# RWKV-7 recurrence feeding a GELU MLP on one core: r's load and transpose are moved, and one chunk's first MLP product changes its tile shape

## The chip, the cores and the metric

The kernel runs on one core of a Trainium2 chip. The metric is the device time of one execution in microseconds; the time of a kernel is the median of several runs. The engines are named as in the profile: PE is TensorE's matmuls and PEld its weight loads, DVE is VectorE, ACT ScalarE, POOL GpSimd, SP SyncE, which here issues nearly all DMAs.

## The reference

For each of 4 batches and 8 heads, a 40x40 state runs through 768 time steps:

```
y[t]  = r[t] @ state
Sa    = state @ a[t]
state = state * w[t] - outer(Sa, b[t]) + outer(v[t], k[t])
```

The 8 heads' y (8 x 40 = 320 columns) become the rows of x, 3072 tokens by 320. Then `h = x @ w_in` (320 to 2048), `g = gelu(h)` with erf, and `out = g @ w_out` (2048 to 320). Everything is float32.

## The kernel before

The 768 steps are cut into 12 chunks, c = 0 to 11, of C = 64 steps. Inside a chunk the recurrence is turned into small matrix products: N and A (a against b and k), M and RV (r against sa and v), an inverse of a unit triangular 64x64 block (a 32x32 part of it on POOL, column by column, L682 and L684; the rest as the products J on PE), X (state against a), saT, and QY (outputs and new state together). All 32 batch and head pairs of a chunk are done at once: 64 products of 40 or 64 rows each, four at a time in 64x64 tiles of the array, or 16 in 32x32 tiles for J.

The order of work is written out by hand. The instructions of each engine run in the order in which the Python code emits them. The loop `for c in range(2, NCH)` at the end of the function is one turn per chunk. In turn c the code finishes chunk c (corner, make_X, joined, make_saT, sa_blocks, make_y2, make_M, make_QY, outputs), prepares chunk n = c + 1 (make_A, make_av, make_RV) and loads and prepares chunk n2 = c + 2 (logs, sums, scale_a, turn_b, turn_r, make_N, the start of its inverse). Turns 3 to 9 have a chunk n2 and take the `else` branches that the diff edits.

Between these steps stand calls of `fill()`. Each runs the next piece of the MLP of the chunk before: mlp(c) is put into the list `pieces` in turn c, so that the first product of mlp(2) is done in turn 3. A chunk's MLP covers 256 tokens (4 batches of 64). The first product, L1043, comes in four pieces, each of 40 matmuls and one GELU over 128x1024 (L1045, ACT):

```
for s in range(2):
    for kt in range(NK):
        for to, end in ((0, HP), (HP, P)):
            for x in range(2):
                matmul(ph[to:end, x, s], w_in_sb[half(x), kt, p*P+to : p*P+end], xt[half(x), kt], ...)
```

NK = 5, HP = 64, P = 128. `half(x)` are the array's upper or lower 64 rows (partitions 0 to 63, 64 to 127), `to` the left or right 64 columns: four 64x64 tiles. Each matmul streams 256 columns. A float32 matmul and its weight load stand in the profile as two records each, so one piece is 80 records and a chunk 320. The second product is L1059 for chunks 0 to 2 and L995 (`seven`, a scheme with seven products of 128x128 tiles) from chunk 3 on; the sums that `seven` needs are DVE work (L1009, L1015, L1016, L999).

What is loaded for chunk n2 in a turn, by SP in this order: w (load_w, 4 DMAs into w_tile, L197), b a second time in the paired form (fetch_pairs "b_turned", 4 DMAs into the a_pairs buffer, L181), r (load_r, 8 DMAs into r_pairs, L178), v (8 DMAs into v_pairs, L178). Then follow the chunk's xt copies (L924, L927), b and k in rows (L163), the inverse's parts (L709, L712), N's store (L620) and its reload for POOL (L674), a and the paired k for the next turn, another copy of v (L217) and the output's stores. b_turned may only start when turn_a has read a_pairs, r when turn_k has read r_pairs, v when turn_v has read v_pairs; these are DVE transposes of 128x1024 (L186). w is read first by logs (ACT's Ln, L425). Within SP a DMA that has to wait holds up all behind it.

turn_r is the DVE transpose r_pairs to rT (L186), from where chunk n2's RV, M and y2 products read it one and two turns later; rT has two buffers. On DVE the turn goes: X's sum (L831), turn_a, turn_k, sa's transpose and 8 copies (L866, L872), the mask of M (L580), turn_v, scale_kT (L547), then the MLP's input xt and the new state (L916, L938, L939), which need QY from PE, then the mask of A, scale_a (L513), turn_b (L186, L522), turn_r, the MLP's sums, the mask of N (L580), L's transpose (L783) and the state's (L952).

Of the kernel before, what the change touches and what calls it, by code (L numbers as in the profile page):

```python
# [19 lines left out]
def kernel(  # L20
# [46 lines left out]
    nc = tc.nc  # L67
    B, H, S, D = r.shape
    DM, DF = moe_w_in.shape
    P = 128  # L70
    C = 64
    HP = 64
# [93 lines left out]
    def fetch_pairs(c, n, src, eng, placed, t=None):  # L166


        if t is None:
            t = paired[n]  # L170
        rows = slice(c * C // 2, (c + 1) * C // 2)
        for x in range(2):
            for z, cols in enumerate((slice(0, D + BL), slice(BL, BW))):
                to = t[x * HP + z * BL:x * HP + (z + 1) * BL, :, :cols.stop - cols.start]
                if placed:
                    for e in range(2):
                        pairs = src[G * e + x].rearrange("h (s y) d -> s h (y d)", y=2)
                        eng.dma_start(out=to[:, e::2], in_=pairs[rows, :, cols])  # L178
                else:
                    pairs = src.rearrange("b (i x) (s y) d -> x s (b i) (y d)", x=2, y=2)[x]  # L180
                    eng.dma_start(out=to, in_=pairs[rows, :, cols])  # L181
        raws[c, n] = t
# [6 lines left out]
    def load_w(c, t=None, eng=nc.sync):  # L189
        t = w_tile if t is None else t  # L190
        to = t[:, :G * DM].rearrange("p (g h d) -> p g h d", g=G, h=H)
        if c < NB:
            fetch(c, "w", w, eng, to)
        else:
            for e in range(2):
                for g in range(G):
                    eng.dma_start(out=to[half(e ^ g), g],  # L197
                                  in_=w[G * e + g, :, c * C:(c + 1) * C].rearrange("h t d -> t h d"))
        raws[c, "w"] = t
# [23 lines left out]
    def load_r(c, eng=nc.sync):  # L223
        if c >= NT:
            fetch_pairs(c, "r", r, eng, True)
            return
        t = by_64(paired["v" if c == 1 else "r"]).rearrange("p (h g) d -> p h g d", g=G)
        for e in range(2):
            for g in range(G):
                eng.dma_start(out=t[half(e), :, g, :D],  # L230
                              in_=r[G * e + g, :, c * C:(c + 1) * C].rearrange("h t d -> t h d"))
        raws[c, "r"] = t
# [311 lines left out]
    def scale_kT(c):  # L544
        t = turned_in[c]
        kT, en = t.pop("k_turned"), t.pop("en")
        nc.vector.tensor_tensor(en, kT, en, ALU.mult)  # L547
        t["kT"] = parts_by_batch(en)
# [485 lines left out]
    def mlp(c):  # L1034
        xt = xts.pop(c)
        for q in range(NF // 4):
            ph = duo("ph").rearrange("p x (s t) -> p x s t", s=2)
            for s in range(2):
                p = 2 * q + s
                for kt in range(NK):  # L1040
                    for to, end in ((0, HP), (HP, P)):
                        for x in range(2):
                            nc.tensor.matmul(ph[to:end, x, s], w_in_sb[half(x), kt, p * P + to:p * P + end],  # L1043
                                             xt[half(x), kt], start=kt == 0, stop=kt == NK - 1)
            nc.scalar.activation(gt[:, 4 * q:4 * q + 4].rearrange("p (x s) t -> p x s t", x=2), ph, ACT.Gelu)  # L1045
            yield
        if c >= NS:
            s1, s2 = half_tile("conv", 2), None
            nc.vector.tensor_tensor(s1, block(1, 0), block(1, 1), ALU.add)  # L1049
            if c >= NCH - 2:  # L1050
                s2 = half_tile("conv", 2)
                nc.vector.tensor_tensor(s2, s1, block(0, 0), ALU.subtract)
            yield from seven(c, s1, s2)
            return
        po = duo("po")[:, :, :DM]
        for part in range(2):
            for g in range(G):
                for f in range(NF // 2 * part, NF // 2 * (part + 1)):
                    nc.tensor.matmul(po[:, g], gt[:, f, g * P:(g + 1) * P], w_out_sb[:, f],  # L1059
                                     start=f == 0, stop=f == NF - 1)  # L1060
                for last in range(G if part and g else 0):
                    os = work.tile([P, DM], FP32, tag="os", name="os", bufs=2)
                    nc.vector.tensor_copy(os, po[:, last])
                    for e in range(2):
                        row = (G * e + last) * S + c * C
                        nc.sync.dma_start(out=out[row:row + C], in_=os[half(e)])
                yield
# [225 lines left out]
    for c in range(2, NCH):  # L1293
        n, n2, n3 = c + 1, c + 2, c + 3
        more, more2, more3 = n < NCH, n2 < NCH, n3 < NCH
        corner(c)
        make_X(c)
        if c > 2:
            turn_blocks(range(4, 16))
        if c == NS + 1:  # L1300
            weight_sums(3)
        if c == 2:

            seconds(1, (14, 14), last=True)
            fill()
            turn_b(n)
            make_N(n)
            run(start_inverse(n, nc.gpsimd))
            store_inverse(n, (nc.gpsimd,))
            load_r(n)  # L1310
            load_v(n)
            load_next(n2)
        else:
            fill()
            if more2:
                load_w(n2)
        joined(c)
        if c == 2:
            pieces.reverse()
            seconds(2, last=True)  # L1320
            fill()
            make_sa(c)
            make_saT(c)
            turn_r(n)
            scale_k(n, nc.vector)
            fill()
            pieces.reverse()
            fill(2)
            turn_k(n)
            load_r(n2)  # L1330
            turn_a(n2)
            fetch_pairs(n2, "b_turned", b, nc.sync, False, paired["a"])
        else:
            if more2:
                turn_a(n2)
                fetch_pairs(n2, "b_turned", b, nc.sync, False, paired["a"])
            if more:
                turn_k(n)
            if more2:
                load_r(n2)  # L1340
            if c == 3:
                scale_b(n)
                scale_k(n, nc.vector)
            fill()
            make_saT(c)
            sa_blocks(c, range(12))
        fill()
        if c > 2:
            sa_blocks(c, range(12, 16))
        make_y2(c)  # L1350
        make_M(c)
        if more:
            turn_v(n)
            if more2:
                load_v(n2)
        if more and c > 2:
            scale_kT(n)
        fill()
        if more2:
            logs(n2)  # L1360
        make_QY(c)
        outputs(c)
        if more2 and c == 2:
            turn_r(n2)
            fetch_pairs(n2, "k_turned", k, nc.sync, False, paired["r"])
        elif more2:
            load_kb(n2)
        pieces.append(mlp(c))
        fill()
        if c == NS:  # L1370
            weight_sums(0)
            weight_sums(1)
        if more:
            make_A(n)
        if more2:
            sums(n2)
        if c > NS:
            fill()
        if more:
            fetch_inverse(n, (0,))  # L1380
            make_av(n)
        if more2:
            scale_a(n2)
            turn_b(n2)
            if c > 2:
                turn_r(n2)
        fill()
        if c == NS:
            weight_sums(2)
        if more2:  # L1390
            make_N(n2)
        if more:
            fetch_inverse(n, (1, 2))
            make_RV(n)
        if more2:
            if c > 2:
                scale_b(n2, nc.gpsimd)
                scale_k(n2, nc.gpsimd)
            steps = start_inverse(n2, nc.gpsimd)
            if more3:  # L1400
                load_a(n3)
            if c == 2:
                load_kb(n2)
            else:
                fetch_pairs(n2, "k_turned", k, nc.sync, False, paired["r"])
            load_VR(n2)
            run(steps)
            store_inverse(n2, (nc.gpsimd,))
        if more:
            if 'early' in ['sm', 'tn']:  # L1410
                turn_within()
                turn_corner(n)
            else:
                turn_corner(n)
                turn_within()
            turn_blocks(range(4))
        fill()
        fill()
# [31 lines left out]
```

## Time and profile before

| | us |
|---|---|
| median of 3 runs (695.57 to 702.57) | 696.25 |
| the profiled execution | 692.65 |
| its span | 690.9 |
| PE busy | 644.9 |
| PEld busy | 557.4 |
| DVE busy | 394.6 |
| POOL busy | 381.9 |
| ACT busy | 286.0 |

The profiled execution's 692.65 us is 1.75 us over its span. The turns of the loop begin with the products X, at 220.2 us for turn 3, 271.1 for turn 4, then 320.5, 370.0, 419.0, 467.3, 516.3 (turn 9), 566.1 and 612.7 (turn 11); they are read from the timeline. The granted clock of TensorE is 1.00 from 200 us to the end. Busy matmul time includes matmuls that overlap each other. "Issue" as a releaser is time in which an engine waited for nothing that the profile shows.

### The profile page before, as it was taken

What the parts mean: (1) busy time and instruction counts of PE and PEld (TensorE: products, weight loads), DVE (VectorE), ACT (ScalarE), POOL (GpSimd) and SP (SyncE); (2) the same over time, 40 slices, a digit from 0 to 9 for tenths busy, and PEclk for the clock granted to TensorE, in tenths of its full rate; (3) what the DMA queues carried; (4) which work ended last, traced back from release to release, by engine and by line L of the source; (5) the groups of instructions that cost most, each with busy time, mean ns of one, the idle gap of its engine ahead of it and who ended that gap; (6) DMA issues with size and microseconds to landing.
All of it is one profiled execution on the core that took longest, in us unless ns stands there. A gap on an engine that the chain in (4) does not pass through costs nothing.

```text
span 690.9 us, 35541 instructions
## 1 busy us (share of the span) xinstructions
PE 644.9 (93%) x16050; PEld 557.4 (81%) x16050; DVE 394.6 (57%) x548; ACT 286.0 (41%) x523; POOL 381.9 (55%) x812
## 2 busy tenths in 40 slices
PE   7578898889999999999999999999999999999997
PEld 4467787657777876898997998997998889979977
DVE  2325779994253774675674684774775765623403
ACT  5223675444143443444445435426526425143020
POOL 5375458820861865855845866875866847820000
PEclk9885899889999999999999999999999999999999
DMA  9698648664658759639649657557657564030100
GB/s 129 109 175 147 128 91 208 139 132 93 124 99 142 130 95 145 116 74 154 123 80 154 127 93 151 112 98 142 116 102 147 104 112 84 23 56 4 39 2 20
DMA packets 287935, 74.64 MB, mean 108 GB/s; under 512 B 265736, under 2 KB 284456, under 8 KB 287784
## 3 DMA queue, kind: packets, MB, share of 16 engines
q1 hardware_dynamic: 283360, 68.20, 54.2%
q0 software_dynamic: 864, 2.36, 2.3%
q8 instruction: 126, 2.06, 1.3%
q10 hardware_dynamic: 3560, 1.80, 1.0%
q14 instruction: 25, 0.20, 0.1%
HBM read 58.69 MB, written 9.70 MB: 99 GB/s over the span
## 4 chain that ended last, share of the span: by engine, by line
PE 73%; POOL 10%; issue 4%; SPq 4%; DVE 3%; DMA 3%; ACT 1%; ACTq 0%; POOLq 0%; DVEq 0%
PE ph L1043 26%; PE po L995 17%; PE po L1059 7%; PE QY L110 6%; POOL W L684 4%; POOL tmp L682 4%; PE J L110 2%; SPq L163 2%; PE sq L110 2%; PE N_ps L110 2%; PE M_ps L110 2%; PE av L110 2%; PE A_ps L110 2%; PE saT_ps L110 2%; PE RV_ps L110 1%
## 5 line engine op out<-in xcount | busy, mean ns | idle before, releaser
L1043 PE MATMUL ph<-xt,w_in_sb 64*64 64x256 f32 x3840 | 222.5, 378 | 5.5 <-issue 5.0
L1043 PEld LDWEIGHTS ph<-xt,w_in_sb 64*64 64x64 f32 x3840 | 169.1, 133 | 41.0 <-issue 9.8
L682 POOL TENSOR_TENSOR tmp<-W,Nb 128x126 f32<-128x126 f32 (+22 forms) x310 | 126.1, 407 | 96.9 <-DMA Nb<-N 73.3
L684 POOL TENSOR_TENSOR W<-W,tmp 128x126 f32<-128x126 f32 (+22 forms) x310 | 133.8, 432 | 24.3
L1045 ACT ACTIVATE gt<-ph 128x1024 f32<-128x1024 f32 x48 | 49.2, 1024 | 108.4 <-PE ph L1043 108.3
L995 PE MATMUL po<-w_out_sb,gt 128*128 128x160 f32 x576 | 84.7, 303 | 0.0
L995 PEld LDWEIGHTS po<-w_out_sb,gt 128*128 128x128 f32 x576 | 78.9, 190 | 4.9 <-issue 3.3
L963 ACT COPY turned<-within 32x256 f32<-32x256 f32 (+3 forms) x144 | 46.3, 322 | 56.0 <-DVE within L952 54.3
L1059 PE MATMUL po<-w_out_sb,gt 128*128 128x320 f32 x192 | 55.7, 447 | 0.0
L1059 PEld LDWEIGHTS po<-w_out_sb,gt 128*128 128x128 f32 x192 | 36.7, 195 | 15.6 <-issue 1.6
L637 POOL TENSOR_TENSOR VR<-VR,upper 128x1024 f32<-128x1024 f32 x8 | 18.9, 2366 | 43.1 <-ACT VR L636 38.4
L916 DVE TENSOR_TENSOR xt<-QY,wpT 128x512 f32<-128x512 f32 x24 | 15.5, 687 | 40.4 <-PE QY L110 40.0
L872 DVE COPY SM<-sa 32x256 f32<-32x256 f32 x72 | 33.5, 465 | 1.2
L814 DVE COPY Tt<-J 32x512 f32<-32x512 f32 x9 | 6.2, 689 | 41.6 <-PE J L110 41.6
L320 ACT ACTIVATE conv<-conv,rebias 128x320 uint32<-128x320 uint32 (+1 forms) x26 | 16.1, 624 | 29.0 <-DVE conv L319 25.9
L995 PE MATMUL po<-extra,half 128*128 128x160 f32 x176 | 26.1, 303 | 0.0
L783 DVE STREAM_TRANSPOSE L<-Tt 128x512 f32<-128x512 f32 x11 | 7.8, 710 | 30.3 <-DMA Tt<-inv 30.3
L866 DVE STREAM_TRANSPOSE sa<-saT 128x1024 f32<-128x1024 f32 x9 | 11.2, 1245 | 23.5 <-ACT saT L856 23.5
L995 PEld LDWEIGHTS po<-extra,half 128*128 128x128 f32 x176 | 24.2, 190 | 0.3
L872 ACT COPY SM<-sa 32x64 f32<-32x64 f32 x72 | 17.4, 242 | 12.8 <-DVE sa L866 11.8
L1049 DVE TENSOR_TENSOR half<-gt 128x1024 f32<-128x1024 f32 x9 | 11.8, 1313 | 18.3 <-ACT gt L1045 18.3
L995 PE MATMUL po<-extra,gt 128*128 128x160 f32 x144 | 21.0, 299 | 0.0
(233 smaller groups left out, 1151.7 us busy)
## 6 DMA issues: line engine op xcount, KB each, us to landing
Nb<-N SPq DMA_DIRECT2D x20, 256.0 KB
VR<-in_v_dram SPq DMA_DIRECT2D x24, 160.0 KB
out_dram<-os SPq DMA_DIRECT2D x48, 80.0 KB
b_rows<-in_b_dram SPq DMA_DIRECT2D x22, 160.0 KB
k_rows<-in_k_dram SPq DMA_DIRECT2D x22, 160.0 KB
N<-N SPq DMA_DIRECT2D x44, 64.0 KB
Tt<-inv SPq DMA_DIRECT2D x44, 64.0 KB
a_pairs<-in_a_dram SPq DMA_DIRECT2D x18, 144.0 KB
```

The source lines that it names most:

```text
L110: nc.tensor.matmul(o, lhsT, rhs, start=first, stop=True, skip_group_check=True)
L320: nc.scalar.activation(power, power, ACT.Relu, bias=rebias, scale=8.0)
L637: nc.gpsimd.tensor_tensor(to, to, upper.unsqueeze(1).to_broadcast([P, 2 * G * NP, C]), ALU.mult)
L682: eng.tensor_tensor(t, W[:, :rows, j:j + 1].to_broadcast([P, rows, rest]), Nb[:, j:j + 1, j + 1:].to_broadcast([P, rows, rest]), ALU.mult)
L684: eng.tensor_tensor(W[:, :rows, j + 1:], W[:, :rows, j + 1:], t, ALU.add)
L872: copy(t["SM"][to:to + BL, g].rearrange("p q m c -> p (q m) c")[:, :, d * BL:end], t["sa"][at:at + BL, :, to:to + end - d * BL])
L916: nc.vector.tensor_tensor(xt[:, :NP, g * P:(g + 1) * P].rearrange("p i (e t) -> p i e t", e=2), Y, wp[:, g, :, :, :C], ALU.mult)
L963: nc.scalar.copy(tn[to:to + deep, :, at:at + wide], within[0][at:at + deep, :, to:to + wide])
L995: nc.tensor.matmul(po[:, n, :DM // 2], l_[:, f], r_[:, f], start=f == 0, stop=f == NF // 2 - 1)
L1043: nc.tensor.matmul(ph[to:end, x, s], w_in_sb[half(x), kt, p * P + to:p * P + end], xt[half(x), kt], start=kt == 0, stop=kt == NK - 1)
L1045: nc.scalar.activation(gt[:, 4 * q:4 * q + 4].rearrange("p (x s) t -> p x s t", x=2), ph, ACT.Gelu)
L1059: nc.tensor.matmul(po[:, g], gt[:, f, g * P:(g + 1) * P], w_out_sb[:, f], start=f == 0, stop=f == NF - 1)
```

## The change

Three edits, and one that only removes a branch never taken (`'early' in ['sm', 'tn']` is false):

1. In mlp, for c == 2 alone, the two 64-column halves of the weights are one matmul of 128 columns: tiles of 64 rows by 128 columns, two of them (x = 0, 1), in place of four of 64x64. The chunk's first product has 160 records in place of 320, and as many fewer weight loads.
2. In turns 3 to 9, the loads are issued in the order r, w, b_turned in place of w, b_turned, r. load_w no longer stands before joined(c).
3. In turns 3 to 9, turn_r(n2) stands behind scale_kT(n), ahead of the MLP's input in DVE's order, in place of behind turn_b(n2).

```diff
@@ mlp
-                    for to, end in ((0, HP), (HP, P)):
+                    for to, end in ((0, P),) if c == 2 else ((0, HP), (HP, P)):
@@ turn c, after make_X
         else:
             fill()
-            if more2:
-                load_w(n2)
         joined(c)
@@
         else:
             if more2:
                 turn_a(n2)
-                fetch_pairs(n2, "b_turned", b, nc.sync, False, paired["a"])
             if more:
                 turn_k(n)
             if more2:
                 load_r(n2)
+                load_w(n2)
+                fetch_pairs(n2, "b_turned", b, nc.sync, False, paired["a"])
@@
         if more and c > 2:
             scale_kT(n)
+            if more2:
+                turn_r(n2)
         fill()
         if more2:
             logs(n2)
@@
         if more2:
             scale_a(n2)
             turn_b(n2)
-            if c > 2:
-                turn_r(n2)
         fill()
@@
         if more:
-            if 'early' in ['sm', 'tn']:
-                turn_within()
-                turn_corner(n)
-            else:
-                turn_corner(n)
-                turn_within()
+            turn_corner(n)
+            turn_within()
             turn_blocks(range(4))
```

In the order of instructions of each engine nothing else moves: POOL and ACT keep theirs, DVE has the one transpose moved in each of the seven turns, SP the eight loads of r put ahead of the eight of w and b. r's first load then waits for turn_k; the waits of the others keep their sources.

## The prediction

> **What bounds the kernel now.** I read the page's engine lines first, then the chain that ended last, then busy time by turn, then the waits of PE, and last the timelines of one turn for PE, DVE and SP.
>
> ```profile
> span 690.9 us, 35541 instructions
> PE 644.9 (93%) x16050; PEld 557.4 (81%) x16050; DVE 394.6 (57%) x548; ACT 286.0 (41%) x523; POOL 381.9 (55%) x812
> ...
> PE 73%; POOL 10%; issue 4%; SPq 4%; DVE 3%; DMA 3%; ACT 1%; ACTq 0%; POOLq 0%; DVEq 0%
> ```
>
> PE is busy for 93% of the span and makes 73% of the chain. The table by turn (columns: length, then busy time per engine, clock, DMA share, GB/s) shows that this holds in every turn that the change touches.
>
> ```profile
> 220.20:271.10 50.90, 49.89 (x1229) 39.79 (x1228) 31.56 (x38) 22.06 (x43) 34.74 (x70) 1.00 0.72 123
> ...
> 370.00:419.00 49.00, 48.29 (x1278) 43.07 (x1276) 31.49 (x43) 23.07 (x47) 34.19 (x70) 1.00 0.70 122
> ...
> 516.30:565.00 48.70, 47.99 (x1209) 42.69 (x1208) 30.11 (x41) 22.79 (x46) 32.77 (x68) 1.00 0.65 120
> ```
>
> PE is idle for 1.0 us of turn 3, 0.7 of turn 6 and 0.7 of turn 9; over turns 3 to 10 (220.2 to 614.0) the same table sums to 384.9 busy of 393.8, so 8.9 us. What can be won by better waits is bounded by that. The waits of PE, first from 220 to 560 us, then to the end:
>
> ```profile
> PE ph L1043 <- issue: 5.0, 6, 1.6
> ...
> PE J L110 <- DVE L L783: 1.7, 2, 1.2
> ```
>
> In the first stretch PE never waits there for DVE, ACT or a load: its largest entry is "issue", in ph. Only at the end, at 566 and 612 us, does it wait for L, which closes POOL's inverse for the last chunks.
>
> The timelines of turn 6 show where the moved transpose lies (DVE) and where the moved loads lie (SP):
>
> ```profile
> 391.45 1.19 DVE L547 TENSOR_TENSOR en<-k_turned,en 128x1024 f32<-128x1024 f32 x1
> 396.44 1.29 DVE L916 TENSOR_TENSOR xt<-QY,wpT 128x512 f32<-128x512 f32 x2 [3.80 <-PE QY L110]
> ...
> 408.40 1.24 DVE L186 STREAM_TRANSPOSE rT<-r_pairs 128x1024 f32<-128x1024 f32 x1
> ...
> 412.03 1.22 DVE L580 TENSOR_TENSOR N<-N_ps,upper 128x1024 f32<-128x1024 f32 x1
> ```
>
> ```profile
> 382.75 3.16 SPq L197 DMA_DIRECT2D w_tile<-in_w_dram  x4
> 386.00 2.17 SPq L181 DMA_DIRECT2D a_pairs<-in_b_dram  x4
> 388.27 4.66 SPq L178 DMA_DIRECT2D r_pairs<-in_r_dram  x8
> 393.02 4.52 SPq L178 DMA_DIRECT2D v_pairs<-in_v_dram  x8
> ```
>
> DVE stands idle for 3.80 us ahead of xt, waiting for QY; SP issues without a gap.
>
> **The change, part by part.** The sum is made against the profiled execution, 692.65 us (span 690.9 and 1.75 around it). The median of the runs shown is 696.25, 3.6 above it; I carry the difference over.
>
> *The 64x128 tiles (turn 3, on the path).* The same product, undisturbed, is seen in the tail, and the dense 128x128 product beside it:
>
> ```profile
> 653.75 17.43 PE ph L1043 x320
> 671.18 15.43 PE po L995 x112
> ```
>
> 320 records in 17.43 us are 54.5 ns each, so four tiles beside one another stream 256 columns in 218 ns, and a chunk has 80 such slots. In the new shape two tiles have to stream the same 256 columns per slot, and there are again 80 slots: half the records, each covering twice the columns of weights. A dense stream of 128x128 tiles takes 15.43/112 = 138 ns for 160 columns, and the po of turn 3 takes 4.50/16 = 281 ns for 320: 0.86 and 0.88 ns per column, 220 and 225 ns for 256. So a slot is 218 to 225 ns if the two row halves run together, 17.4 to 18.0 us for the chunk, +0 to +0.6; I take +0.1, since the 64x64 row is the nearest (same operands, same row halves). A gain below 218 isn't shown by any row; as a lower end I take -0.2.
>
> The neighbours of these four pieces (X, saT, y2 with M, QY) stay in 64x64 tiles, so the array's shape now changes six more times: after X, before and after saT, before y2, after M, before QY (the J after the first piece changes it anyway). What a change costs is read from equal groups of 64 records in the chain:
>
> ```profile
> 300.48 1.09 PE A_ps L110 x64
> 301.57 0.95 PE wT_ps L110 x64
> ...
> 320.47 1.08 PE X L110 x64
> ```
>
> A_ps follows a 128x128 product, X follows 32x32 tiles, wT_ps follows 64x64 tiles: 0.13 to 0.14 us per change. Six are +0.8. Bounds: 0, if matmul ends hide it, and 1.9, by the gap that J2 makes in turn 3 (the first piece ends at 225.61, the next begins at 226.98, less 0.75 for 64 records of J: 0.31 per change).
>
> *turn_r ahead of xt.* Seven transposes of 1.24 us move into the idle time between en's end and xt's start: 3.47, 3.33, 3.54, 3.80, 3.27, 3.72 and 4.04 us in turns 3 to 9, all over 1.24. That costs nothing while r has landed. In the trace r's eight loads land 7.2 us after the first is issued in turn 6 (388.27 to 395.45). Issued at w's old time, 382.75, they land at 390.0; en ends at 392.64. In turn 9 it is 529.91 + 6.3 = 536.2 against 539.09, in turn 8 487.5 against 490.11. The old reader of that rT buffer, M, is masked on DVE before. Without that cover, xt, the state and X would be late by what r is late beyond about 2.1 us, the room that is left. At its old place the transpose frees 1.2 us ahead of the MLP's sums and N's mask. PE waits for neither: m3 starts right behind RV. The mask comes earlier by up to 1.2 us where DVE was late with it (turn 4: N_ps is done at 312.1, the mask starts at 313.41), but N's store on SP then waits for the fetch of Tt ahead of it: it gains 1.1 us in turn 4, 0.3 in turn 6, nothing in turns 7 to 9, where the store comes 1.7 to 2.5 us behind the mask. What of that reaches the wait for L at the end I put at -0.2 (bounds -1.7, the whole wait, and 0).
>
> *r ahead of w and b on SP.* The same 16 issues; w and b each go out 4.7 to 5.9 us later, the length of r's issues. w landed at 388.05 in turn 6, now at about 392.7; Ln starts at 395.86. In turn 9 it is 537.94 + 4.7 = 542.6 against 542.28, so Ln is 0.3 us late, and behind it on ACT stand the table load and the exponentials, which wait for wT on PE; wT (546.7) has 3.7 us of room behind Ln's end. b lands at 544 instead of 539.5 there, and turn_b starts at 552.6. r's first load now waits for turn_k with w, b, v, xt and N's store queued behind it: SP gets to it after turn_k's end in all turns but turn 4 (280.52 against 282.43, 1.9 us), where SP before stood 1.4 us at v (292.21 to 293.57). The net 0.5 us delays xt's copies, which landed at 309.7 for a use at 321.6. v's place is unchanged. Cost 0 (bounds 0 and +1.5, if that delay and Ln's reached PE).
>
> *PE's instructions.* The stops in ph called "issue" come at 274.6, 323.9, 377.8, 422.5, 475.2 and 519.9, shortly after the short J and X products; the page's instruction queue moves 126 packets, 2.06 MB. 320 records fewer in turn 3 shift where those packets' ends fall in every later turn. The trace doesn't show in which direction: from -5.0, all of the stops gone, to +5.0, twice as many. I take 0.
>
> Sum: 0.1 + 0.8 - 0.2 + 0 + 0 = +0.7, so 693.35 us for an execution like the profiled one and 696.25 + 0.7 = 696.95, about 697.0, for the median. The likeliest case's own range is 693.5 to 700: the bounds of tiles and switches (-0.2 to +2.5), half of the issue term (2.5 each way), and the runs' own scatter.
>
> **The rivals.**
>
> *Weight loads exposed (slower).* With only two tiles, a load may find its own rows still streaming. The load of 128 columns is 190 ns (L995), of 64 columns 133 (L1043). If the difference of 57 ns shows in each slot, 80 x 0.057 = +4.6 us; if the whole load shows, 80 x 0.19 = +15.2; if the halves don't run beside each other at all, 160 x 0.22 - 17.4 = +17.8. The time would be near 708 (middle of 701 to 715). It ends beyond 1% from 87 ns per slot on. Against it: 128x128 tiles, with one tile alone, take 138 ns per record though each load's row is 190, so a load does run beside a matmul of its own rows. The Trainium skill ("TensorE: Matmul & The Clock Gate", Part 3, "What overlaps and what doesn't") says that weight loads overlap with running matmuls only if the row group differs; the same page's load time of columns over 1.2 GHz would by that make an estimated 128/1.2 = 107 ns exposed per slot, 80 x 0.107 = +8.5 us. The 138 ns just named disagree, and the measurement decides. Chance 0.11.
>
> *r is late (slower).* If the loads of r, now between the output's stores and w, land more than 2.1 us after en's end, DVE stands before xt, and QY's results wait: at most 1.24 us of transpose and as much wait in seven turns, about +9 to +12 us, 707. For it: DMA engines are 65 to 72% busy in these turns. Against it: 2.6 to 4.7 us of margin before the idle time is even used. Chance 0.05.
>
> *PE's stops fall away (faster).* If the shifted packets remove the 5.0 us of issue and the earlier N the 1.7 us at the end, 696.25 + 0.9 - 6.7 = 690.5. For it: the stops come in the same two places of the turn, 41 or 25 records into a piece. Against it: the burst of short products before them stays. Chance of at least half of that: 0.15.
>
> *The change does nothing measurable on DVE and SP.* That is inside the likeliest case, since I count both near 0.
>
> **How the numbers follow.** The likeliest case has 0.69, exposed loads 0.11, late r 0.05, stops gone 0.15. The range reaches down to 690.5, the full third rival, and up to 704, the lower third of the exposed loads: left out are about 0.10 above and 0.05 below. More than 1%, about what a measurement of this kernel tells from no change, is 7 us: below 689.3 or above 703.2. Faster by that needs all of PE's idle waits, 0.05; slower has most of the first two rivals, 0.12; the same 0.83.
>
> **What would show it.** Right: ph of mlp(2) in 160 records and 17.2 to 18 us in turn 3, with saT and X at about 1.1 us there instead of 0.95; turns 4 to 9 of 48 to 50 us as before; rT directly behind en, with xt still released by QY; N's mask about 1.2 us earlier behind nT in turns 4 to 9; w landing about 5 us later, with Ln delayed at most in turn 9. Wrong: a piece of ph of 6 us or more, DVE idle ahead of rT for r_pairs, wT waiting for w_tile, or the entry "issue" in ph changed by more than 3 us.

## The result and the profile after

The changed kernel takes 703.09 us (median of 22 runs, 696.60 to 707.69), beside 699.28 for the kernel before on the same chip (22 runs, 695.57 to 706.09). The ratio is 1.0048, with a 95% interval of 1.0027 to 1.0070: some 3.4 us slower, where +0.7 was forecast. The ratio leaves out executions more than 1.5% above the fastest of their kernel (three of the 22 of the changed one), so it lies a little under the quotient of the two medians, 1.0054. The kernel before moved between 695.7 and 699.3 from one set of runs to the next, so from here on only ratios inside one set are compared.

The profiled execution of the changed kernel took 703.61 us; its span, 701.8 us, is 10.9 us longer than that of before. Of that, 5.8 us lie ahead of turn 3, which begins at 226.0 us instead of 220.2, in code that the change does not touch. In the profiles below this stretch took 221 to 230 us whatever the kernel. What is left, 5.1 us from turn 3 to the end, is what the two traces can be asked about.

The page after, its engines and the releasers of the chain:

```profile
span 701.8 us, 35208 instructions
PE 653.8 (93%) x15890; PEld 562.9 (80%) x15890; DVE 395.1 (56%) x548; ACT 286.5 (41%) x523; POOL 387.2 (55%) x812
...
PE 64%; SPq 9%; POOL 8%; DMA 6%; DVE 5%; issue 4%; ACT 3%; ACTq 0%; DVEq 0%; POOLq 0%
```

160 matmul records fewer, and yet PE is busy for 8.9 us longer, 5.1 of them ahead of turn 3. In the chain, SP's queue rises from 4% to 9% and DMA from 3% to 6%: something outside PE has begun to set the end of turns. The table by turn (turns 3 to 9 and the rest; length, busy time of PE, PEld, DVE, ACT and POOL, clock, DMA share, GB/s):

```profile
226.00:278.40 52.40, 50.97 (x1080) 40.77 (x1068) 31.75 (x38) 22.16 (x43) 34.65 (x70) 1.00 0.70 122
278.40:326.40 48.00, 47.94 (x1280) 42.22 (x1276) 33.20 (x42) 22.79 (x46) 34.42 (x70) 1.00 0.67 113
326.40:374.00 47.60, 47.56 (x1278) 43.20 (x1274) 29.95 (x37) 21.18 (x42) 32.68 (x68) 1.00 0.65 120
374.00:424.90 50.90, 47.82 (x1278) 41.98 (x1272) 31.12 (x42) 22.79 (x46) 36.71 (x71) 1.00 0.66 119
424.90:474.00 49.10, 49.00 (x1284) 43.99 (x1274) 31.15 (x42) 22.78 (x46) 34.11 (x71) 0.97 0.67 120
474.00:525.40 51.40, 48.10 (x1280) 43.26 (x1274) 31.74 (x43) 22.79 (x47) 37.09 (x73) 0.99 0.65 118
525.40:575.30 49.90, 49.90 (x1278) 44.25 (x1272) 31.24 (x41) 22.78 (x46) 32.90 (x70) 0.94 0.67 118
575.30:701.80 126.50, 120.01 (x2456) 106.31 (x2448) 47.04 (x77) 35.62 (x80) 31.29 (x67) 0.99 0.17 35
```

Turn 3 is 1.5 us longer than before (50.9). Turns 4 and 5 take 48.0 and 47.6, 3.3 less than before (49.4 and 49.5), with PE idle for less than 0.1 us in each. Then it turns around: turn 6 has 3.1 us of idle PE (0.7 before), turn 8 has 3.3 (0.9 before), and turns 7 and 9 have no idle time but more busy time, at a lower clock (0.97, 0.94). The 5.1 us by this table: PE's busy time is +1.1 in turn 3, +3.4 in turns 7 and 9 and the last stretch, -0.6 in the others, together +3.85; its idle time is +1.25. The idle time as a whole hardly changed, but its kind did. The waits of PE, from 220 to 560 us and then to the end:

```profile
PE J L110 <- DVE L L783: 5.9, 2, 3.0
...
PE wT_ps L110 <- ACT w_tile L425: 0.4, 2, 0.2
```

```profile
PE J L110 <- DVE L L783: 2.2, 1, 2.2
```

The entry "issue" in ph, 5.0 us before, is gone. In its place stands the wait for L: 8.1 us in all, 1.7 before. The timeline of DVE in turn 6 answers to the one shown of before:

```profile
395.84 1.19 DVE L547 TENSOR_TENSOR en<-k_turned,en 128x1024 f32<-128x1024 f32 x1
397.16 1.25 DVE L186 STREAM_TRANSPOSE rT<-r_pairs 128x1024 f32<-128x1024 f32 x1
399.18 1.29 DVE L916 TENSOR_TENSOR xt<-QY,wpT 128x512 f32<-128x512 f32 x2 [0.77 <-PE QY L110]
...
411.51 1.28 DVE L1015 TENSOR_TENSOR gt<-gt,SM 128x1024 f32<-128x1024 f32 x1
412.71 1.29 DVE L1016 TENSOR_TENSOR gt<-gt 128x1024 f32<-128x1024 f32 x1
...
414.16 1.21 DVE L580 TENSOR_TENSOR N<-N_ps,upper 128x1024 f32<-128x1024 f32 x1
423.39 0.71 DVE L783 STREAM_TRANSPOSE L<-Tt 128x512 f32<-128x512 f32 x1 [8.03 <-DMA Tt<-inv]
```

rT lies behind en, and QY still releases xt. N's mask starts 40.2 us into the turn (42.0 before). L, though, comes 49.4 us into it, and PE can only start the next turn behind it. In before's turn 6, which begins at 370.0, L comes 46.0 us into it:

```profile
415.97 0.71 DVE L783 STREAM_TRANSPOSE L<-Tt 128x512 f32<-128x512 f32 x1 [2.72 <-DMA Tt<-inv]
```

### The profile page after: what moved, and what is told of

Its sections match the earlier page's. It is cut to its first block, busy times and chain, and to the rows that moved or that the text cites. A ratio compares the mean times of both kernels' runs of the same rounds, so it can differ in the third digit from the quotient of the medians.

```text
span 701.8 us, 35208 instructions
## 1 busy us (share of the span) xinstructions
PE 653.8 (93%) x15890; PEld 562.9 (80%) x15890; DVE 395.1 (56%) x548; ACT 286.5 (41%) x523; POOL 387.2 (55%) x812
## 4 chain that ended last, share of the span: by engine, by line
PE 64%; SPq 9%; POOL 8%; DMA 6%; DVE 5%; issue 4%; ACT 3%; ACTq 0%; DVEq 0%; POOLq 0%
PE ph L1043 22%; PE po L995 12%; PE po L1059 7%; PE QY L110 5%; POOL W L684 4%; POOL tmp L682 4%; SPq L163 2%; PE J L110 2%; PE sq L110 2%; DMA inv<-W 2%; PE N_ps L110 1%; PE X L110 1%; PE av L110 1%; DMA Tt<-inv 1%; PE M_ps L110 1%
## 5 line engine op out<-in xcount | busy, mean ns | idle before, releaser
L1043 PE MATMUL ph<-xt,w_in_sb 64*64 64x256 f32 (+1 forms) x3680 | 222.4, 383 | 0.2
L1043 PEld LDWEIGHTS ph<-xt,w_in_sb 64*64 64x64 f32 (+1 forms) x3680 | 168.4, 138 | 37.1 <-issue 3.8
L682 POOL TENSOR_TENSOR tmp<-W,Nb 128x126 f32<-128x126 f32 (+22 forms) x310 | 128.0, 413 | 102.7 <-DMA Nb<-N 79.1
L684 POOL TENSOR_TENSOR W<-W,tmp 128x126 f32<-128x126 f32 (+22 forms) x310 | 137.5, 444 | 24.3
L783 DVE STREAM_TRANSPOSE L<-Tt 128x512 f32<-128x512 f32 x11 | 7.8, 711 | 49.4 <-DMA Tt<-inv 49.4
L580 DVE TENSOR_TENSOR N<-N_ps,upper 128x1024 f32<-128x1024 f32 x12 | 14.6, 1220 | 12.6 <-PE N_ps L110 12.6
```

Source lines behind the costliest of these rows:

```text
L682: eng.tensor_tensor(t, W[:, :rows, j:j + 1].to_broadcast([P, rows, rest]), Nb[:, j:j + 1, j + 1:].to_broadcast([P, rows, rest]), ALU.mult)
L684: eng.tensor_tensor(W[:, :rows, j + 1:], W[:, :rows, j + 1:], t, ALU.add)
```

## The experiments

The first question was which part costs the time. "Before" and "after" stand ahead of each diff for the kernel that is edited.

**The tiles alone.** Before, with the one line:

```diff
-                    for to, end in ((0, HP), (HP, P)):
+                    for to, end in ((0, P),) if c == 2 else ((0, HP), (HP, P)):
```

> Before, with only mlp(2)'s first product in 64x128 tiles. Theory P (PE paces the turns, but SP's issue queue has no spare time, so what PE gains in one turn comes back as a wait for L some turns later): the whole difference is here, ratio 1.003 to 1.006 against before; turn 3 longer by about 1.4 us, the 5 us of issue in ph gone, waits of J for L of 3 us and more with half-clock windows behind them. Rival Q (the order of loads costs): only turn 3's 1.4 us, ratio 1.002 or less, no waits for L before turn 10.

Measured: ratio 1.0003 (0.9976 to 1.0030). The same kernel in a second set:

> The tiles alone once more, since their first measurement (1.0003, interval 0.998 to 1.003) stands beside 1.005 for each kernel with the tiles and one of the moves. If the tiles are what costs, 1.003 to 1.006; if the moves are needed for the loss, 1.000 to 1.002.

Measured: 1.0041 (1.0008 to 1.0074). The intervals overlap between 1.0008 and 1.0030. Both profiles show what the changed kernel shows: "issue" in ph falls to at most 0.5 us, turns 4 and 5 take 95.4 and 96.3 us together (98.9 before), and PE then waits for L (first and second set, up to 560 us):

```profile
PE J L110 <- DVE L L783: 4.1, 3, 2.8
```

```profile
PE J L110 <- DVE L L783: 3.1, 3, 1.7
```

To the end it is 6.8 and 6.5 us, beside 1.7 in before. So in both profiles the tiles alone trade PE's stops for waits for L.

**Both moves, then each alone.** Before, with edits 2 and 3 of the change, then with one of them:

> Before, with r loaded ahead of w and b and turn_r ahead of xt, tiles as before. Theory P: 1.000, within 0.2%, the issue stops in ph stay at about 5 us and N's store lags its mask by no more than before. Rival Q: 1.003 or more, with SP's busy time per turn up by 1 to 2 us and N's store 4 us or more behind its mask.

Measured: 1.0015 (0.9986 to 1.0044). The stops stay, and up to 560 us there is no wait for L:

```profile
PE ph L1043 <- issue: 4.9, 5, 1.3
```

> Before, with turn_r alone moved ahead of xt, loads in the old order w, b, r. r's last part landed 2.8 us behind en in turn 6, so the transpose should now wait for r_pairs. Theory P: xt is late by up to 0.5 us in some turns, N's mask 1 us earlier, ratio 0.999 to 1.002. A theory by which the transpose itself costs on the path: 1.24 us x 7, 1.012.

Measured: 0.9991 (0.9966 to 1.0015).

> Before, with r's loads alone moved ahead of w and b, turn_r in its old place. Theory P: 1.000 within 0.2%. Rival Q: as large as the moves together, 1.003 or more, since it is SP's order that costs.

Measured: 1.0010 (0.9984 to 1.0036). Neither move shows an effect of its own on the time. The stops in ph are 6.2 and 2.3 us in these two profiles, with PE's instructions as in before: their sum varies by that much without the tiles.

**The changed kernel again.**

> The changed kernel once more, timed beside before and beside the three kernels below. If the three edits only add to one another, the parts measured alone (tiles 1.0003, moves 1.0015) put it at 1.002; if they work on the same spare time of SP's queue, it stays near 1.005. Theory P expects the second, with issue in ph below 1 us, waits of J for L of 4 us or more between 220 and 560 us, and N's store 3 to 6 us behind its mask from turn 5 on.

Measured: 1.0054 (1.0023 to 1.0086), with 5.2 us of waits for L up to 560 us (8.3 to the end) and no "issue" in ph. The loss is confirmed.

**The tiles with one move.** Before, with the tiles and turn_r moved, loads in the old order:

> Tiles and turn_r's move, loads in the old order. If the order of loads is what joins with the tiles to make the loss, this is 1.000; if any of the two moves will do, or none is needed, 1.003 to 1.005.

Measured: 1.0054 (1.0026 to 1.0083), and as slow as the full change by another way. DVE waits for r, and in turn 7 PE waits for what stands behind it (waits of DVE, then its timeline and that of PE):

```profile
DVE rT L186 <- DMA r_pairs<-in_r_dram: 22.3, 5, 7.2
```

```profile
457.48 1.25 DVE L186 STREAM_TRANSPOSE rT<-r_pairs 128x1024 f32<-128x1024 f32 x1 [7.22 <-DMA r_pairs<-in_r_dram]
```

```profile
460.56 1.99 PE L110 MATMUL wT_ps<-cum_m,w_tile 64*64 64x64 f32 x64 [3.39 <-DVE st L938]
```

That is the rival "r is late", made real where r is loaded behind w and b. With turn_r alone DVE waited for r too, for 4.6 us, at no measurable cost. In the change as made the new load order keeps it away.

> Tiles and the new order of loads, turn_r in its old place. Theory P (SP's queue is full, and the new order delays N's store when PE runs without its issue stops): 1.004 to 1.006, N's store 3 us and more behind its mask. If the order of loads doesn't matter, as the tiles alone: 1.000.

Measured: 1.0050 (1.0028 to 1.0073), with 3.0 us of waits for L up to 560 us (5.8 to the end). The three kernels with the tiles and at least one move lie between 1.0048 and 1.0054 in four measurements; the tiles alone lie at 1.0003 and 1.0041.

**Where the tiles stand.** If the stops go because fewer instructions shift where PE's instruction packets end, the same tiles in turn 7 must leave the stops of turns 3 to 6 and remove those behind. Before, with:

```diff
-                    for to, end in ((0, HP), (HP, P)):
+                    for to, end in ((0, P),) if c == 6 else ((0, HP), (HP, P)):
```

> Before, with the 64x128 tiles in chunk 6 (turn 7) in place of chunk 2. If the tile's price lies in its own turn, turn 7 has four pieces of 4.5 us and more and is some 1.4 us longer. If fewer PE instructions ahead are what ends the issue stops in ph, the stops of turns 4 to 6 (3 to 4 us) stay and those after turn 7 go; if they end for another reason, they go everywhere or nowhere. Ratio 1.000 to 1.004.

Measured: 1.0020 (0.9990 to 1.0050). The waits of PE up to 421 us (two of the entries), then from 471 to 621:

```profile
PE ph L1043 <- issue: 3.2, 4, 1.7
PE J L110 <- DVE L L783: 0.4, 1, 0.4
```

```profile
PE J L110 <- DVE L L783: 2.9, 3, 1.9
```

The second answer has no entry "issue" in ph. The first half of the expectation held: with the tiles out of turn 3 the stops of turns 4 to 6 are back. That the tiles removed those behind turn 7 is not shown. PE waited for L ahead of each of turns 7 to 10, at turn 7 even before the tiles ran, and before has no stop in ph in the two turns that begin with such a wait either (10 and 11).

**Is SP's queue what delays L?** SP issues for 42 to 48 us of a turn in the changed kernel (43 to 45 before), and N's store comes 0.0 to 5.9 us behind the end of N's mask (0.0 to 2.5 before). First, after, with v's eight loads issued by ACT at the same place in the code:

```diff
-            fetch_pairs(c, "v", v, nc.sync, True)
+            fetch_pairs(c, "v", v, nc.scalar if c > NS + 1 else nc.sync, True)
```

> The changed kernel with the eight loads of v issued by ACT in place of SP in turns 3 to 9, where ACT stood idle for some 4.5 us ahead of its last GELU. It takes some 4.5 us of issue per turn off SP. Theory P: N's store follows its mask at once, J no longer waits for L, no half-clock windows after 226 us, turns of 47 to 48 us, ratio to before 0.985 to 0.995. If SP's queue is not what delays L, the waits for L stay and the ratio is 1.003 to 1.007.

Measured: 1.0291 (1.0255 to 1.0326). N's store comes with its mask, but ACT stands at the loads, since v may only start when turn_v has read the old one, and GELU and Ln are queued behind them:

```profile
355.45 5.49 ACTq L178 DMA_DIRECT2D v_pairs<-in_v_dram  x8
360.99 1.02 ACT L1045 ACTIVATE gt<-ph 128x1024 f32<-128x1024 f32 x1 [7.91 <-DMA v_pairs<-in_v_dram]
```

```profile
PE wT_ps L110 <- ACT w_tile L425: 15.8, 5, 3.7
```

The test decided nothing on SP, because it put a bigger wait in place of the one it removed. The next two put v's loads behind make_RV(n), where turn_v is long done (for c > 2), on ACT, once in before and once in after, with the edit of load_v above and:

```diff
             if more2:
-                load_v(n2)
+            if more2 and c == 2:
+                load_v(n2)
...
             make_RV(n)
+            if more2 and c > 2:
+                load_v(n2)
```

> Before, with v's eight loads in turns 3 to 9 issued by ACT behind the copy of RV, where ACT is idle for 5 us, in place of SP. Theory P: N's store at once behind its mask in all turns; PE is then alone on the path, with its issue stops of about 5 us: 0.995 to 0.999. If ACT's issues hold up the copies of the state's transpose behind them, 1.003 or more.

Measured: 1.0016 (0.9981 to 1.0051), with 3.6 us of waits for L to the end, 1.7 in before.

> The changed kernel with v's loads issued by ACT behind the copy of RV. Theory P: no wait of J for L before turn 10, no half-clock windows between 230 and 600 us, turns 4 to 9 of 47.5 to 48.5 us: 0.988 to 0.997 against before, 1% and more below the changed kernel. If something else than SP's queue makes L late, the waits stay and it is 1.003 or more.

Measured: 1.0029 (0.9996 to 1.0061), with 3.4 us of waits for L up to 560 us (6.3 to the end). SP's busy time per turn fell to 36 to 40 us in both, and N's store still came 1.4 to 4.9 us behind its mask in the first and 2.9 to 4.8 in the second. The waits of SP in the second and its timeline in turn 6 say why:

```profile
SPq L709 <- DMA inv<-W: 33.8, 7, 6.6
```

```profile
409.71 1.89 SPq L163 DMA_DIRECT2D k_rows<-in_k_dram  x2
415.35 2.02 SPq L709 DMA_DIRECT2D Tt<-inv  x2
417.94 1.94 SPq L620 DMA_DIRECT2D N<-N  x4
```

SP now stands idle before L709, the fetch of Tt, which waits for POOL's inverse to land; N's store is queued behind that fetch. The theory that SP has too much to issue fell in this form: taking issues away did not bring N's store to its mask. What binds in this kernel is the order of that queue: the store of the next chunk's N waits for the inverse of this one, in all seven turns, and POOL's inverse starts every 48.5 to 49.7 us. In the changed kernel itself the same waits of SP hold only one short entry for it (230 to 570 us):

```profile
SPq L709 <- DMA inv<-W: 0.5, 1, 0.5
```

There SP's own issues (xt's copies, b and k in rows, Tt) fill nearly all the time between N's mask and its store. So both hold N's store back, the issues ahead of it and the wait for the inverse, and where the first are taken away the second remains.

No kernel here is shown to be faster than the kernel before.

## Why the prediction was right or wrong

**The direction and the range held; the size did not.** +0.7 was forecast, some +3.4 (1.9 to 4.9) measured. That the sign came out is partly luck: the +0.7 was made of the tiles and the shape changes, and the loss came from a wait that the sum had at -0.2 and from a clock that it did not have. Two of the prediction's own signs of being right or wrong went against it: "issue" in ph changed by 5.0 us, and turns 5, 6 and 8 took 47.6, 50.9 and 51.4 us instead of 48 to 50. Three terms were mis-sized.

*The tiles.* The row halves do run side by side, and "weight loads exposed" is dead. The chain in turn 3:

```profile
227.18 4.52 PE ph L1043 x40
...
232.38 4.52 PE ph L1043 x40
236.90 1.15 PE saT_ps L110 x62
...
242.56 1.09 PE QY L110 x64
```

Twenty slots in 4.52 us are 226 ns each, just over the 218 to 225 of the prediction; the chunk takes 18.1 us, +0.6 where I took +0.1. The nearest row was the dense 128x128 product (225), not the 64x64 tiles whose operands it shares. The rule of the Trainium skill ("TensorE: Matmul & The Clock Gate", Part 3, "What overlaps and what doesn't") by which the load shows when the row group does not differ, an estimated +8.5 us, is not what these 226 ns show. saT at 1.15 and y2 (the QY of 1.09) are 0.1 to 0.2 us longer behind a change of shape, as forecast, but the sum of +0.8 for six changes is not there: from the start of X to the end of QY the stretch takes 25.88 us, and 25.71 in before with a stop of 0.50 in it. Tiles and changes together thus cost +0.7, where +0.9 was forecast. The turn as a whole measured +1.1 us of busy time and +1.5 of length; most of the length lies behind QY, where PE now stops for 0.64 us in RV and waits 0.35 us for A.

*PE's stops.* "I take 0" failed. The term in ph was -5.0, the end of its bounds, in this trace and nearly so in every one with the tiles in turn 3 (at most 0.5 us left); the instruction queue moves 125 packets for 126. The place of a stop follows the instructions ahead of it: in all six profiles in which PE's instructions are the same up to turn 4, turn 4 has a stop of 0.8 to 2.0 us ahead of the same record of ph, 39 before the end of its piece, and seven of the eight with the tiles in turn 3 have one of 0.4 to 1.7 us in RV of turn 3 instead, where before has none. That the ends of the instruction packets are what moved was not shown, and in later turns the sum differs between profiles of the same instructions (2.3 to 6.2 us).

*What reaches the wait for L.* This is the step that failed. It was put at -0.2, with bounds of -1.7 and 0, and measured +6.4 us (8.1 for 1.7), because it was read from a trace in which PE was late itself. When the stops go, PE's turn falls to 47.6 to 48.0 us, and a second loop, of nearly the same length, sets the pace:

1. N's mask on DVE, N's store on SP, its reload Nb (L674), POOL's 30 to 34 us of inverse, its store, the fetch of Tt, L.
2. The next N's store stands in SP's queue behind that fetch.

The timeline of SP in turn 6 of the changed kernel shows it:

```profile
415.36 2.37 SPq L163 DMA_DIRECT2D b_rows<-in_b_dram  x2
417.82 1.75 SPq L163 DMA_DIRECT2D k_rows<-in_k_dram  x2
420.17 0.87 SPq L709 DMA_DIRECT2D Tt<-inv  x2
421.13 2.07 SPq L620 DMA_DIRECT2D N<-N  x4
...
425.51 1.95 SPq L674 DMA_DIRECT2D Nb<-N  x2
```

N's mask ended at 415.37; its store goes out at 421.13, its reload at 425.51. In this turn SP is through with b and k at 419.57 and waits 0.5 us for the inverse. So the mask, earlier by the moved transpose, gains nothing: the prediction had seen that for turns 7 to 9, and stopped there. Two short turns put POOL behind PE, and from the end of turn 6 on PE waits for L, at the end of every second turn.

*The rival "PE's stops fall away"* (0.15) had its first half right, and the wrong time: the stops went, but the wait for L, which it took away too, grew. Its 690.5 us held only if nothing else was due at the same moment.

**What the sum did not have at all: POOL's inverse and the clock.** POOL's inverse became a little longer, a mean of 31.7 us instead of 30.7 in turns 4 to 9: where it comes late in PE's turn, its last columns meet DVE's nT and the MLP's sums, which with the transpose gone from between them stand 1.2 us closer (timeline of POOL in turn 6; the second column is the duration):

```profile
410.20 0.30 POOL L684 TENSOR_TENSOR W<-W,tmp 128x56 f32<-128x56 f32 x1
410.58 1.13 POOL L682 TENSOR_TENSOR tmp<-W,Nb 128x45 f32<-128x45 f32 x1
411.79 1.14 POOL L684 TENSOR_TENSOR W<-W,tmp 128x45 f32<-128x45 f32 x1
413.00 1.10 POOL L682 TENSOR_TENSOR tmp<-W,Nb 128x30 f32<-128x30 f32 x1
414.18 0.25 POOL L684 TENSOR_TENSOR W<-W,tmp 128x30 f32<-128x30 f32 x1
```

Three short operations take 1.1 us each while DVE runs nT (410.35), L1015 (411.51) and L1016 (412.71); the same 128x45 columns took 0.26 and 0.27 us in before's turn 6. The Trainium skill ("GPSIMD Engine Reference", § 8. Key points) says that POOL shares its SBUF interfaces with VectorE, with contention for DVE instructions that have two SBUF inputs; the trace agrees, at some 0.9 us for each such meeting here. Turns 4 to 9 have 28 POOL operations of the inverse stalled in this way, 21 before. The kernels with the moved transpose and no tiles have 17, those with the tiles and the transpose in its old place 28, 24 and 25: the count goes with how late POOL lies in PE's turn, not with the transpose.

And each of the three waits for L, of 2.2 to 3.0 us, is followed by a stretch at half clock (timeline of PE at the first of them, then stretches ahead of, in and behind it, with the granted clock as the third number from the end):

```profile
424.25 0.74 PE L110 MATMUL J<-L,N 32*32 32x32 f32 x64 [2.90 <-DVE L L783]
424.93 1.84 PE L110 MATMUL X<-st,aT 40*64 40x40 f32 x64
426.53 5.50 PE L1043 MATMUL ph<-xt,w_in_sb 64*64 64x256 f32 x80
```

```profile
424.00:425.10 1.10, 0.85 (x76) 0.84 (x77) 1.10 (x2) 0.00 (x0) 1.04 (x3) 1.00 0.61 96
425.10:428.50 3.40, 3.40 (x84) 2.76 (x84) 2.37 (x7) 3.13 (x8) 0.14 (x2) 0.50 0.69 134
428.50:431.00 2.50, 2.50 (x52) 1.74 (x50) 0.00 (x0) 2.40 (x10) 0.23 (x1) 1.00 1.02 203
```

X and the piece of ph behind it take about 1.5 us longer; the same happens at 524 and 623 us, and the table by turn gives +3.4 us of busy time for the three together. Before's profile has no such stretch from turn 3 on; its waits for L were 0.5 and 1.2 us. Over that part of the profiles, one execution each, half clock was granted for 0 us in before, 3.4 with both moves, 6.8 and 17.1 with the tiles alone, 13.7 and 17.1 in the changed kernel, 3.4 in it with v late. The tiles alone were thus nearly free in the set whose profile shows 6.8 us (1.0003) and not in the other (1.0041). But 6.8 us also stand beside 1.0010 (the load order alone) and 1.0050 (the tiles with it), so single profiles do not settle the price. Every run records its mean granted clock over the whole execution. Its median is 0.956 to 0.958 for before in three sets, 0.949 and 0.950 for the changed kernel, 0.951 for it with v late, 0.954 and 0.951 for the tiles alone, 0.952 and 0.953 for the tiles with one move, and 0.955 to 0.959 for the moves without the tiles. So with the tiles in turn 3 it is lower than before's in the same set, clearly so except in the first set of the tiles alone. That agrees with the clock as part of the price and does not prove it.

**What was right.** rT directly behind en, with QY still releasing xt; Ln late by little ("wT" waits 0.4 us in all for w_tile); no wait of PE for r; the loads at 0. "The change does nothing measurable on DVE and SP" is what the runs with the moves alone show (0.9991 to 1.0015).

**What stays open.** The tiles alone came out at 1.0003 and 1.0041, with the moves at 1.005; whether the moves add to the loss, or the tiles make it all, the intervals do not settle. How much of the loss is idle time, the clock or POOL was not separated. Nor was the loop itself cut: a kernel with N's store ahead of Tt's fetch was not tried.

## What to carry to other kernels

When an engine is busy for 93% and its waits are short, look for a second loop of nearly the same period before crediting the removal of stops: here PE's turn of 48 to 49 us hid one of 49 to 51 us through POOL, SP's queue order and two DMAs, and whatever PE won came back as a wait for it. Price such a wait with what follows it, here 2 to 3 us of idle PE and then 1 us or more lost at half clock. A term whose bounds are wide on both sides (±5.0) should not be carried as 0 without saying what is late next at each end of it.

## What the runs showed of the hardware

- 64x128 tiles in float32: 226 ns for a slot of two matmuls that stream 256 columns side by side, against 218 ns for four 64x64 tiles in before's tail.
- In the changed kernel, waits of TensorE of 2.2, 2.9 and 3.0 us were each followed by 3.4 to 6.8 us at a granted clock of 0.50. With the tiles in turn 7 a wait of 0.94 us was, and in before one of 1.19 us was not, so no length of wait that is safe can be read from here.
- A POOL operation of 0.3 us takes 1.1 us when a DVE operation of 128x1024 with two SBUF inputs falls on it.
- The stops of PE that the profile calls "issue" depend on the PE instructions ahead of them: in six profiles with the same instructions a stop of 0.8 to 2.0 us comes ahead of the same record of turn 4, and in the eight with 160 matmul records fewer in turn 3 at most 0.5 us of such stops is left in ph, where the others have 2.3 to 6.2.
